# Induced attention with a max-out layer: the softmax over tokens moved ahead, its maxima sent through DRAM, its sums kept running

## The chip, the core and the metric

The kernel runs on one core of a Trainium2 chip. That core has five engines with a queue of their own each: TensorE (PE in the profile; its weight loads are listed apart as PEld), VectorE (DVE), ScalarE (ACT), GpSimd (POOL) and SyncE (SP). SP issues every DMA of this kernel, strictly in the order of its queue. All numbers are device microseconds (us) of one execution; less is better.

## The reference

`x` holds 4 batches of 12544 tokens with 128 channels, `inducing` 32 vectors of 128 channels. Cut to what is computed:

```
scale = 1 / sqrt(128)
# phase 1, one batch: 32 induced rows look at all 12544 tokens
s = scale * (inducing @ x.T);  a = softmax(s, over the tokens);  h = a @ x        # h: 32 x 128
# phase 2, every token looks at the 32 rows
s = scale * (x @ h.T);         p = softmax(s, over the 32 rows); y = p @ h
# max-out layer
z = max(y @ w1, y @ w2, y @ w3)                                                   # 768 wide
out = z @ w_out
```

All of it is float32.

## The kernel before

**Tiles.** A batch is 98 tiles of 128 tokens: one short group (group 0) of 2 tiles and six full groups (1 to 6) of 16. The four partition quarters of 32 hold four tiles side by side, so a group's 32 x tokens scores fill one PSUM bank of 128 x 512.

**Phase 1 of a group** (`attend_...`, lines 256 to 334): scores of the induced rows into `bank_a[1]` (L263, four products that sit in four column quarters of TensorE); the negated maximum of each partition on VectorE (L273); the four quarters' maxima are brought together by ScalarE (a 128x4 column, L280) and a small TensorE product with `sel` (L287), and VectorE takes the least (L291); then exp with its sum (L297, ScalarE), a 32x32 transpose (L311, VectorE), sixteen small products with the token tiles `xg` (L321) and a copy to `hg` (L334, ScalarE). Each group has a maximum of its own. After the seventh group the groups are rescaled and joined: L402 to L412, the product of the sums (L439), one product for each group (L423), the quotient (L443 to L449), and then U, which is the state times the weight differences `wcat` (L490, two banks, two column halves). U is split into a high and a low part and put into rows by four DMAs (L510); it is `us` below.

**Phase 2 of a group** (`scores_products`, `scores_steps`): scores (L525) into `bank_a[0]`, and ten steps on VectorE and ScalarE to the probabilities `ph` and `pl`, which DMAs (L591) put into `pT`, four for each chunk of 512 tokens.

**The main loop** goes over 600 slots: 4 batches x 25 chunks (a short one of 256 tokens, then 24 of 512) x 6 blocks of the 768 wide layer. A slot has two products for the layer (L606 into `pu`, L612 into `pv`), a relu on ScalarE (L621), a maximum on VectorE (L639), a rounded copy `hi` on ScalarE (L628), the rest `lo` on GpSimd or, in a few slots, on VectorE (L636, L642), and six slots later three products with `w_out` (L662 to L664). The first slot of a chunk has one more (L661), the last is followed by a copy and a DMA out (L669, L670).

**What sets the order.** All engines are ordered by hand. `at(s, f, ...)` puts a call into `plan[s]`, and `main` runs slot by slot: `advance()` (layer products), the `pT` loads, the copy out, the plan of the slot, then `stage2`. So work that is planned between two slots stands in each engine's queue exactly there. A window is 24 slots, the four chunks of a full group; window g of batch b starts at slot `150 b + 6 + 24 (g - 1)`. In the main loop of batch b the plan interleaves phase 2 of the next group and phase 1 of batch b + 1: at slots 2 and 15 of a window TensorE gets a burst of the products for both (the functions `burst` and `softmax1` set the steps, `LATE` shifts some of them by 12 slots). In windows 1 and 4 two groups of phase 1 are started, in windows 2, 3 and 5 one; in window 5 the groups are joined, and window 6 has the first phase 2 scores of the next batch. Phase 1 of batch 0 runs ahead of the loop, with its own order (`phase1_first`).

Tokens come as `xg` (L91) and, for batches 1 to 3, also as channels `xT` (L102); the short group's are `xgs` and `xTs`. They are tiles from rotating pools.

## Time and profile before

| what | value |
|---|---|
| median of 3 runs | 843.29 us (843.27 to 844.43) |
| profiled execution: span from the first to the last instruction | 841.7 us |
| what lies around the span, against the median run | 1.6 us |
| TensorE busy in the span | 817.0 us (97%) |
| ScalarE, GpSimd, VectorE busy | 741.3, 635.4, 630.7 us |
| before the first slot of the main loop | 56.5 us |
| mean granted TensorE clock | 0.995 |

The page gives no time of the profiled execution other than its span; the runs' median is 1.6 us longer. How to read it: busy shares are means over stages, and matmuls are pipelined, so that a busy TensorE says little by itself. The chain of waits follows the work that ended last back to its start; where it runs through TensorE without a break, each piece of it is time that TensorE was given for one instruction before the next could start.

### The profile page before, as it was taken

To read this page: it belongs to the slowest core of one execution; us is meant where nothing else is said; L and a number is where in the kernel's file an instruction comes from. 1 tells how busy PE (TensorE), PEld (TensorE's weight loads), DVE (VectorE), ACT (ScalarE), POOL (GpSimd) and SP (SyncE) were. 2 spreads that over 40 slices of the span, in tenths; PEclk is the share of its full clock that TensorE was granted. 3 is DMA by queue.
4 is the path that set the end of the run, shared out by engine and by line. 5 is a ranking of instruction groups with operands and counts; after the bars stand their busy time and mean duration, and the time that the engine had idled before them with its cause. 6 is when DMAs were issued, how large, how long until landed. Compare 5 with 4: busy or idle time off the path is not lost.

```text
span 841.7 us, 14677 instructions
## 1 busy us (share of the span) xinstructions
PE 817.0 (97%) x4608; PEld 635.9 (76%) x4608; DVE 630.7 (75%) x1076; ACT 741.3 (88%) x1547; POOL 635.4 (75%) x512
## 2 busy tenths in 40 slices
PE   6879999999999999999999999999999999999998
PEld 4647778777787777777777777877768878778786
DVE  5868778777686777777787778777868778777864
ACT  5759889898798998988799889889879999999996
POOL 0039778778597787877778878878759888888887
PEclk9989999999999999999999999999999999999999
DMA  9734624433425345244332462432222222222221
GB/s 348 267 96 155 219 76 157 169 116 103 146 66 175 126 157 173 70 164 158 114 92 76 162 216 70 163 122 58 64 77 81 79 75 69 64 70 76 72 79 51
DMA packets 42717, 102.50 MB, mean 122 GB/s; under 512 B 8976, under 2 KB 11152, under 8 KB 37392
## 3 DMA queue, kind: packets, MB, share of 16 engines
q1 hardware_dynamic: 42640, 101.57, 37.3%
q8 instruction: 37, 0.61, 0.3%
q14 instruction: 40, 0.33, 0.1%
HBM read 48.12 MB, written 25.69 MB: 88 GB/s over the span
## 4 chain that ended last, share of the span: by engine, by line
PE 92%; DMA 3%; DVE 2%; ACT 1%; issue 1%; SPq 0%; ACTq 0%; DVEq 0%
PE acc L662 17%; PE acc L663 16%; PE acc L664 16%; PE pu L606 16%; PE pv L612 16%; PE acc L661 3%; PE aux L525 3%; PE acc L321 2%; DMA xg<-in_x_dram 2%; PE aux L263 2%; DMA xTs<-in_xt_dram 1%; PE aux L490 1%; PE aux L423 1%; ACT ru L621 0%; PE acc L287 0%
## 5 line engine op out<-in xcount | busy, mean ns | idle before, releaser
L636 POOL TENSOR_TENSOR lo<-h,hi 128x512 fp32r<-128x512 f32 (+1 forms) x498 | 629.5, 1296 | 153.6 <-ACT hi L628 100.5
L639 DVE TENSOR_TENSOR h<-pv,ru 128x512 f32<-128x512 f32 (+1 forms) x600 | 404.5, 675 | 188.0 <-PE pv L612 122.6
L621 ACT ACTIVATE ru<-pu 128x512 f32<-128x512 f32 (+1 forms) x600 | 375.8, 626 | 73.8 <-PE pu L606 70.7
L628 ACT CAST hi<-h 128x512 fp32r<-128x512 f32 (+1 forms) x600 | 386.9, 645 | 0.3 <-DVE h L639 0.3
L662 PE MATMUL acc<-hi,wo_hi 128*128 128x512 f32 (+1 forms) x600 | 238.4, 397 | 0.0
L606 PE MATMUL pu<-pT,us 128*128 128x512 f32 (+1 forms) x600 | 232.7, 388 | 3.4 <-ACT hi L628 1.2
L612 PE MATMUL pv<-pT,us 128*128 128x512 f32 (+1 forms) x600 | 233.4, 389 | 0.0
L663 PE MATMUL acc<-hi,wo_lo 128*128 128x512 f32 (+1 forms) x600 | 232.0, 387 | 0.0
L664 PE MATMUL acc<-lo,wo_hi 128*128 128x512 f32 (+1 forms) x600 | 231.8, 386 | 0.0
L662 PEld LDWEIGHTS acc<-hi,wo_hi 128*128 128x128 f32 x600 | 113.2, 189 | 43.0 <-issue 22.0
L606 PEld LDWEIGHTS pu<-pT,us 128*128 128x128 f32 x600 | 113.2, 189 | 26.9 <-POOL us L479 2.0
L612 PEld LDWEIGHTS pv<-pT,us 128*128 128x128 f32 x600 | 113.4, 189 | 23.8 <-DVE h L639 1.3
L664 PEld LDWEIGHTS acc<-lo,wo_hi 128*128 128x128 f32 x600 | 113.0, 188 | 23.0
L663 PEld LDWEIGHTS acc<-hi,wo_lo 128*128 128x128 f32 x600 | 113.3, 189 | 20.6
L642 DVE TENSOR_TENSOR lo<-h,hi 128x512 fp32r<-128x512 f32 x102 | 72.4, 710 | 0.8 <-ACT hi L628 0.8
L669 ACT COPY o<-acc 128x512 f32<-128x512 f32 (+1 forms) x100 | 61.6, 616 | 3.1 <-PE acc L664 3.1
L661 PE MATMUL acc<-pT,us 128*128 128x512 f32 (+1 forms) x100 | 38.7, 387 | 0.0
L321 PEld LDWEIGHTS acc<-xg,aT 128*32 128x32 f32 x768 | 20.5, 110 | 13.9 <-ACT ru L621 5.7
L219 POOL TENSOR_TENSOR wo_lo<-wf,wo_hi 128x768 fp32r<-128x768 f32 x1 | 1.8, 1809 | 37.5 <-ACT wo_hi L218 37.5
L263 PE MATMUL aux<-xT,iT 128*32 128x512 f32 x192 | 25.9, 596 | 1.6 <-ACT xT L255 1.6
L321 PE MATMUL acc<-xg,aT 128*32 128x128 f32 x768 | 25.8, 274 | 1.5 <-DVE aT L311 1.1
L525 PE MATMUL aux<-xT,hT 128*32 128x512 f32 x192 | 25.6, 604 | 0.0
(101 smaller groups left out, 438.6 us busy)
## 6 DMA issues: line engine op xcount, KB each, us to landing
out_dram<-o SPq DMA_DIRECT2D x96, 256.0 KB, 2.0
xg<-in_x_dram SPq DMA_DIRECT2D x23, 1024.0 KB, 7.3
xT<-in_xt_dram SPq DMA_DIRECT2D x18, 1024.0 KB, 5.3
pT<-ph SPq DMA_DIRECT2D x192, 64.0 KB, 2.0
pT<-pl SPq DMA_DIRECT2D x192, 64.0 KB, 2.0
raw<-in_w_dram SPq DMA_DIRECT2D x3, 768.0 KB, 12.0
us<-uh SPq DMA_DIRECT2D x6, 208.0 KB, 3.1
us<-ul SPq DMA_DIRECT2D x6, 208.0 KB, 3.7
```

The costliest lines, as they stand in the source:

```text
L321: nc.tensor.matmul(out=hps[q * M : (q + 1) * M, :C], lhsT=aT[:, t * M : (t + 1) * M], rhs=xg[:, t, :], start=(t < NQ), stop=(t + NQ >= nt),)
L606: nc.tensor.matmul(out=pu[:, :w], lhsT=state[c.b]["us"][:, 2 * j * P : (2 * j + 1) * P], rhs=c.pT[:, :w], start=True, stop=True)
L612: nc.tensor.matmul(out=pv[:, : d.w], lhsT=state[d.b]["us"][:, (2 * j + 1) * P : (2 * j + 2) * P], rhs=d.pT[:, : d.w], start=True, stop=True,)
L621: nc.scalar.activation(out=ru[:, :w], in_=pu[:, :w], func=AF.Relu)
L628: nc.scalar.copy(out=hi[:, : c.w], in_=h[:, : c.w])
L636: nc.gpsimd.tensor_sub(**args)
L639: nc.vector.tensor_max(out=h[:, : d.w], in0=pv[:, : d.w], in1=relus.pop(s)[:, : d.w])
L642: nc.vector.tensor_sub(**low)
L661: nc.tensor.matmul(out=c.acc[:, :w], lhsT=us[:, 2 * DF :], rhs=c.pT[:, :w], start=True, stop=False)
L662: nc.tensor.matmul(out=c.acc[:, :w], lhsT=wo_hi[:, j, :], rhs=c.hh[j][:, :w], start=False, stop=False)
L663: nc.tensor.matmul(out=c.acc[:, :w], lhsT=wo_lo[:, j, :], rhs=c.hh[j][:, :w], start=False, stop=False)
L664: nc.tensor.matmul(out=c.acc[:, :w], lhsT=wo_hi[:, j, :], rhs=c.hl[j][:, :w], start=False, stop=(j == NJ - 1))
```

## The change

- **Phase 1 is one loop of turns.** A turn is a group; the short group and group 1 are one turn (`turns`), so there are six turns for each batch. For batch 1 they start in windows 0, 0, 1, 1, 2 and 3 of batch 0 (`FIRST`, counted from 0). For batches 2 and 3 they start one in each window, beginning in the last window but one of the batch two ahead. The products of the states and U of a batch come in the last window but one ahead of it.
- **Maxima.** VectorE negates the scores into SBUF and takes their least in one instruction (L381). The 128 values of four bytes go to a DRAM tile by one DMA (L400) and are fetched from there by another (L407), so that every partition gets four; VectorE takes the least of them and of the least so far (L413). The ScalarE column and the TensorE product with `sel` are gone for batches 1 to 3.
- **Running sums.** A turn's sums are added to `hs` and `ls` on VectorE after a rescaling by `fac` (L425 on ScalarE, L458 to L470). At the end two small products remain (L477, L478).
- **U in one bank.** Four products in four column quarters, 416 wide (L635), then one copy and one subtraction, and sixteen DMAs of 32 rows in place of four of 64 (L656). The short group's scores share that bank (L673).
- **Tiles.** `xT` and `xg` are fixed tiles with free lists, eight and five of them; the constants, `wcat` and the short group's channels are places in one tile, `shelf`. For batches 2 and 3 the `xT` loads are planned 11 slots ahead of their products; token loads go out at slot 17 of the window ahead of the sums.

```diff
-    LATE = 12
+    turns = [(0, 1)] if groups[0]["nt"] < GT else [(0,), (1,)]
+    turns += [(gi,) for gi in range(2, NG)]
...
+    short_t = [place(groups[0]["nt"] * P) for i in range(2)]
+    iT = place(M)
...
+    def turn_products(b, k):
+        for gi in turns[k]:
+            w = groups[gi]["nt"] * M
+            bank = bank_a[1] if groups[gi]["nt"] == GT else spare[0][:, C : C + w]
...
+    def turn_max(b, k):
...
+            nc.vector.tensor_scalar(
+                out=a[:, at : at + w],
+                in0=bank,
+                scalar1=-1.0,
+                scalar2=None,
+                op0=ALU.mult,
+                op1=ALU.min,
+                accum_out=mq[:, i : i + 1],
+            )
...
+    def turn_send(b, k):
+        far = st[("mq", k)] = dp.tile([P], F32, name="far", tag="far"), st.pop(("mq", k))
+        nc.sync.dma_start(out=far[0].rearrange("(m q) -> q m", q=NQ), in_=far[1])
+    def turn_fetch(b, k):
+        far = st.pop(("mq", k))[0]
+        every = far.rearrange("(m q) -> m q", q=NQ).unsqueeze(0).to_broadcast([NQ, M, NQ])
+        nc.sync.dma_start(out=st["mm"][:, k, :NQ], in_=every)
+    def turn_least(b, k):
+        nc.vector.tensor_reduce(out=st["mm"][:, k + 1, NQ:], in_=st["mm"][:, k, :known], axis=AX.X, op=ALU.min)
+    def turn_weights(b, k):
+        nc.scalar.activation(out=a, in_=a, func=AF.Exp, bias=least, scale=-1.0, accum_out=st["lst"][:, k : k + 1])
+        if k > 0:
+            nc.scalar.activation(
+                out=st["fac"][:, k : k + 1], in_=st["mm"][:, k, NQ:], func=AF.Exp, bias=least, scale=-1.0
+            )
...
+    def turn_keep(b, k):
+        if k == 0:
+            nc.vector.tensor_copy(out=st["hs"], in_=st["h"])
+            return
+        fac = st["fac"][:, k : k + 1]
+        nc.vector.scalar_tensor_tensor(
+            out=st["hs"], in0=st["hs"], scalar=fac, in1=st["h"], op0=ALU.mult, op1=ALU.add
+        )
...
+    def turn_totals(b, bank):
+        nc.tensor.matmul(out=st["lp"], lhsT=st["ls"].to_broadcast([P, P]), rhs=sel[:, :M], start=True, stop=True)
+        nc.tensor.matmul(out=st["sum"], lhsT=st["hs"], rhs=sel[:, :M], start=True, stop=True)
...
-        for k in range(2):
+        for k in range(NQ):
             nc.tensor.matmul(
-                out=bank[k * 2 * M : (k + 1) * 2 * M, :n],
-                lhsT=st["hT"][:, : 2 * M],
-                rhs=wcat[:, k * UH + half * n : k * UH + (half + 1) * n],
+                out=st["up"][k * M : (k + 1) * M, :],
+                lhsT=st["hT"][:, :M],
+                rhs=wcat[:, k * UQ : (k + 1) * UQ],
...
+    def turn(b, k, s):
+        at(s, turn_products, b, k)
+        at(s + 2, turn_max, b, k)
+        at(s + 4, turn_send, b, k)
+        at(s + 11, turn_fetch, b, k)
+        at(s + 19, turn_least, b, k)
+        at(s + 20, turn_weights, b, k)
+        at(s + 22, turn_transpose, b, k)
...
+    FIRST = ((0, 0), (0, 1), (1, 0), (1, 1), (2, 0), (3, 0))
+    BURST = (2, 15)
+    LOADT = ((0, 0, 0), (0, 0, 1), (0, 5, 2), (0, 15, 3), (1, 16, 4), (2, 15, 5))
+    LOADX = ((0, 4, 0), (0, 17, 1), (1, 4, 2), (1, 17, 3), (2, 17, 4), (3, 17, 5))
...
+            else:
+                i, part = NW * (n - 2) + NW - 2 + k, 0
+                then = (i + 1, part)
+                if k == 0:
+                    at(window(i - 1) + 7, start_batch, n)
+                at(window(i - 1) + 15, load_channels, n, k)
+                at(window(i) + 17, load_tokens, n, k)
+            at(window(then[0]) + BURST[then[1]], turn_sums, n, k)
+            at(window(then[0]) + BURST[then[1]] + 1, turn_keep, n, k)
+        s0 = window(NW * n - 2)
+        at(s0 + 6, turn_totals, n, bank_a[1])
...
+        at(s0 + 15, combine_products, n, bank_a[1])
+        at(s0 + 15, scores_products, n, 0, bank_a[1][:, UQ : UQ + 2 * M])
...
+        for r in range(NQ):
+            at(s0 + 18 + 2 * r, combine_rows, st, r)
```

How the order of the engines moves, at the places where the prediction counts. In the rows `xnn` counts equal instructions in a row, and `shelf` after the change stands for `iT`, `sel`, `wcat` and the short group's `xTs`.

**SP where a batch begins.** Before, at the start of batch 1, window 1 (SP, slots 0 to 6):

```order
L670 DMA out_dram<-o 128x512
L102 DMA xTs<-in_xt_dram 128x256
L102 DMA xT<-in_xt_dram 128x2048
L591 DMA pT<-ph 32x512
L591 DMA pT<-pl 32x512
L591 DMA pT<-ph 32x512
L591 DMA pT<-pl 32x512
L102 DMA xT<-in_xt_dram 128x2048
L670 DMA out_dram<-o 128x256
```

Now the same two loads, for batch 2, stand in the window ahead of the one that uses them (SP, slots 6 to 18 of the fourth window of batch 0; L400 is the send of the maxima, L407 their fetch, L820 the DMA out, L741 the `pT` loads):

```order
L400 DMA far<-mq 4x32x1
L741 DMA pT<-ph 32x512
L741 DMA pT<-pl 32x512
L741 DMA pT<-ph 32x512
L741 DMA pT<-pl 32x512
L820 DMA out_dram<-o 128x512
L407 DMA mm<-far 128x1x4
L106 DMA shelf<-in_xt_dram 128x256
L106 DMA xT_90<-in_xt_dram 128x2048
L741 DMA pT<-ph 32x512
L741 DMA pT<-pl 32x512
L741 DMA pT<-ph 32x512
```

The two loads have moved from the slot just ahead of their products to 11 slots ahead; a send and a fetch have been put between the DMAs of each turn.

**TensorE where the states of a batch are joined.** Before (PE, slots 15 to 17 of the fifth window of batch 0; L606 and L612 are the layer's products, L662 to L664 those with `w_out`):

```order
L321 MATMUL acc_86<-xg,aT 32x128 x16
L662 MATMUL acc_85<-hi,wo_hi 128x512
L663 MATMUL acc_85<-hi,wo_lo 128x512
L664 MATMUL acc_85<-lo,wo_hi 128x512
L606 MATMUL pu_82<-pT,us 128x512
L612 MATMUL pv_83<-pT,us 128x512
L439 MATMUL acc_86<-sel,l_2633 128x32
L662 MATMUL acc_85<-hi,wo_hi 128x512
L663 MATMUL acc_85<-hi,wo_lo 128x512
L664 MATMUL acc_85<-lo,wo_hi 128x512
L606 MATMUL pu_81<-pT,us 128x512
L612 MATMUL pv_84<-pT,us 128x512
```

Now (PE, slot 6 of the same window; L756 and L762 are the layer's products, L811 to L814 those with `us` and `w_out`):

```order
L756 MATMUL pu_81<-pT,us 128x512
L762 MATMUL pv_82<-pT,us 128x512
L477 MATMUL aux_79<-shelf,ls 128x32
L478 MATMUL aux_79<-shelf,hs 128x32
L811 MATMUL acc_85<-pT,us 128x512
```

The product of the sums stood one slot behind the last group's sums, in the bank that L334 reads; now two products stand four slots behind them, in `bank_a[1]`, and the seven products of L423 are gone.

**TensorE in a burst.** Now, slot 2 of the fifth window of batch 0 (PE; the first turn of batch 2):

```order
L673 MATMUL aux_78<-xT_91,hT 32x512 x4
L446 MATMUL acc_85<-xg_95,aT 32x128 x16
L363 MATMUL acc_85<-shelf 32x64 x4
L363 MATMUL aux_79<-xT_90,shelf 32x512 x4
L812 MATMUL acc_84<-hi,wo_hi 128x512
```

Scores of phase 2 (L673), the sums of the turn before (L446) and the next turn's scores (L363) stand in one burst, the short group's with them; before, the short group's stood in bursts of their own ahead of group 1's. Over the main loop TensorE has 26 bursts with such products now and had 32.

More of the change, by code (lines that the diff above doesn't have):

```diff
@@ L50 @@
     UW = 2 * DF + C
-    UH = UW // 2
+    UQ = UW // NQ
     groups = []
@@ L105, with place @@
     xg_next = {}
-    iT = const.tile([P, M], F32, name="iT")
+    xts_free = [const.tile([P, GT * P], F32, name=f"xT{i}", tag=f"xT{i}") for i in range(XTB)]
+    xgs_free = [const.tile([P, GT, C], F32, name=f"xg{i}", tag=f"xg{i}") for i in range(XB)]
+    w_space = xts_free.pop()
+    shelf = const.tile([P, UW + 2 * groups[0]["nt"] * P + 2 * P + 2 * M], F32, name="shelf")
+    shelf_at = [0]
+    def place(n):
+        shelf_at[0] += n
+        return shelf[:, shelf_at[0] - n : shelf_at[0]]
+    short_t = [place(groups[0]["nt"] * P) for i in range(2)]
+    iT = place(M)
     def load_raw(src):
@@ L121, in first_loads @@
                 raws.append(load_raw(srcs[what - NG]))
-    ident = const.tile([P, P], F32, name="ident")
+    ident = place(P)
     make_identity(nc, ident)
@@ L126 @@
     nc.vector.tensor_copy(out=ident_r, in_=ident)
-    sel = const.tile([P, P], F32, name="sel")
+    sel = place(P)
     nc.vector.tensor_reduce(
@@ L334, in attend_keep @@
         nc.scalar.copy(out=st["hg"][:parts, gi, :], in_=st["h"][:parts, :C])
+    def turn_products(b, k):
+        st = state[b]
+        banks = {}
+        for gi in turns[k]:
+            w = groups[gi]["nt"] * M
+            bank = bank_a[1] if groups[gi]["nt"] == GT else spare[0][:, C : C + w]
+            for q in range(NQ):
+                nc.tensor.matmul(
+                    out=bank[q * M : (q + 1) * M, :w],
+                    lhsT=iT,
+                    rhs=st["xT"][gi][:, q * w : (q + 1) * w],
+                    start=True,
+                    stop=True,
+                )
+            banks[gi] = bank[:, :w]
+        st[("s", k)] = banks
@@ new lines, in turn_max @@
+    def turn_max(b, k):
+        st = state[b]
+        a = wk.tile([P, WK], F32, name="a", tag="a")
+        mq = wk.tile([P, 2], F32, name="mq", tag="mq")
+        at = 0
+        for i, (gi, bank) in enumerate(st.pop(("s", k)).items()):
+            w = bank.shape[1]
+            nc.vector.tensor_scalar(
[7 more added lines that the diff above has]
+            )
+            at += w
+        if len(turns[k]) > 1:
+            nc.vector.tensor_tensor(out=mq[:, :1], in0=mq[:, :1], in1=mq[:, 1:], op=ALU.min)
+        st[("a", k)] = a[:, :at]
+        st[("mq", k)] = mq[:, :1]
@@ new lines, in turn_sums @@
+    def turn_sums(b, k):
+        st = state[b]
+        aT = st.pop(("aT", k))
+        rows = [st["xg"][gi][:, t, :] for gi in turns[k] for t in range(groups[gi]["nt"])]
+        for gi in turns[k]:
+            xg = st["xg"].pop(gi)
+            if groups[gi]["nt"] == GT:
+                xgs_free.append(xg)
+        st["h"] = spare[0][:, :C]
+        for t, row in enumerate(rows):
+            q = t % NQ
+            nc.tensor.matmul(
+                out=st["h"][q * M : (q + 1) * M, :],
+                lhsT=aT[:, t * M : (t + 1) * M],
+                rhs=row,
+                start=(t < NQ),
+                stop=(t + NQ >= len(rows)),
+            )
@@ L536, in scores_steps @@
         flat = sp[:, :w]
+        if nt < GT:
+            flat = wk.tile([P, w], F32, name="es", tag="es", bufs=1)
         ev = flat.rearrange("p (t m) -> p t m", m=M)
-        nc.vector.transpose(out=flat, in_=flat)
+        nc.vector.transpose(out=flat, in_=sp[:, :w])
         yield
@@ L795, in main @@
+    for n in range(1, B):
+        for k in range(NK):
+            i, part = FIRST[k] if n == 1 else (NW * (n - 2) + NW - 2 + k, 0)
+            turn(n, k, window(i) + BURST[part])
     def main():
```

227 lines of the change are left out of this document (106 added, 121 removed).

## The prediction

> **What bounds the kernel now.** I read the page's head and its chain first, then the stretches of the batches, then the chain piece by piece, then the waits.
>
> ```profile
> span 841.7 us, 14677 instructions
> PE 92%; DMA 3%; DVE 2%; ACT 1%; issue 1%; SPq 0%; ACTq 0%; DVEq 0%
> ```
>
> ```profile
> core 0: us, PE busy (x) PEld busy (x) DVE busy (x) ACT busy (x) POOL busy (x), PEclk, DMA share, GB/s
> 460.00:661.00 201.00, 198.24 (x1124) 154.25 (x1123) 151.05 (x260) 178.92 (x377) 158.71 (x127) 1.00 0.35 111
> 661.00:841.70 180.70, 177.16 (x802) 141.67 (x800) 135.19 (x214) 168.07 (x329) 149.56 (x116) 1.00 0.23 70
> ```
>
> The chain is TensorE for 92% of the span. Batch 2 takes 201.0 us, the last one 180.7: it runs the same layer but has no next batch whose phase 1 it must carry. So phase 1 of a batch costs about 20 us inside the loop, and the change lies in three such stretches. TensorE is idle for 2.8 us of the 201.0, so nearly everything must come from the length of TensorE's own queue, and little from waits.
>
> ```profile
> 206.32 0.23 PE pv L612
> 206.56 1.01 PE acc L321 x32
> 207.57 0.43 PE acc L662
> ...
> 210.07 0.41 PE acc L439 x2
> ...
> 211.69 1.51 PE aux L423 x14
> 213.20 0.28 PE acc L662
> ...
> 216.93 1.55 PE aux L490 x8
> 218.48 0.43 PE acc L662
> ```
>
> These are pieces of the chain (start, us). A layer product is worth 0.23; the first one behind a burst 0.43, so a burst pays 0.20 beyond its own pieces. (A product of float32 counts twice in `x`.)
>
> ```profile
> 122.83 1.00 PE aux L525 x8
> 123.83 0.87 PE acc L321 x32
> 124.70 0.86 PE aux L263 x8
> 125.56 0.43 PE acc L662
> ...
> 172.59 1.01 PE acc L321 x32
> 173.60 0.86 PE aux L263 x8
> ...
> 269.41 0.12 PE acc L287 x2
> 269.53 0.34 PE acc L662
> ...
> 293.49 1.08 PE acc L321 x32
> ```
>
> With the 0.20: a burst of all three costs 1.00 + 0.87 + 0.86 + 0.20 = 2.93, one of two 1.01 + 0.86 + 0.20 = 2.07. So a member that joins a burst costs 0.86, while sums alone cost 1.01 + 0.20 = 1.21: a burst as such costs about 0.34. The row at 293 is a burst whose transpose came late: 1.08 - 0.87 = 0.21 more.
>
> ```profile
> PE acc L439 <- ACT hg L334: 3.4, 3, 1.1
> PE aux L263 <- DMA xTs<-in_xt_dram: 2.9, 2, 1.5
> ```
>
> These are TensorE's two real stalls in the loop (us, times, longest): it waits for ScalarE's copy where a batch is joined, and for the short group's channels where a batch begins.
>
> **The change part by part.** All terms are for batches 1 to 3, as phase 1 of batch 0 keeps its code.
>
> *Channels loaded earlier.*
>
> ```profile
> DMA to landing us min/median/max: 2.3/2.5/2.6
> ```
>
> That is `xTs`. The load that was late stands 11 slots ahead now, some 13 us at 29.3 / 24 = 1.2 a slot (the last row of the windows below), against 2.5 us to land. The stall of 2.9 us goes.
>
> *Running sums.* The product of the sums no longer waits for L334; it reads what VectorE made three slots before. 3.4 us go. What could be late next is VectorE there; I allow up to 0.5 us twice in the range.
>
> *Maxima through DRAM.* 21 products with `sel` go, 0.12 + (0.34 - 0.23) = 0.23 each: 4.8 us. The two DMAs of a turn cost TensorE nothing as long as they are hidden; that cover is worked out under the third rival.
>
> *Joining.* The products of the groups go: 1.51 + 0.28 - 0.23 = 1.56, three times: 4.7 us. One small product comes for it. Two of the fourteen pieces of L423 would be 0.22; the piece of L439 as a whole, 0.41, bounds it from above. I take 0.22: 0.7 us back.
>
> *U in one bank.* Now 1.55 + 0.20 = 1.75. The new form is four column quarters as in L263, whose eight pieces take 0.86 at 512 wide; at 416 wide 0.70 in proportion. With 0.20 that is 0.90, so 0.85 less, 2.5 us for three; if it costs as much as at 512, 2.1. The short group's scores that now stand with it left another burst, which is no difference.
>
> *Fewer bursts.* 26 in place of 32, counted in the order: 6 x 0.34 = 2.0 us. Six bursts of the 293 kind, two in each batch, come from transposes at slot 25; all turns behind a full burst now transpose at slot 24, as in the row at 122.83: 6 x 0.21 = 1.3 us. (A second turn in a window is followed by its sums a whole window later.)
>
> *ScalarE and VectorE.* They are next in line, so their loads decide whether TensorE's shorter queue is worth its length.
>
> ```profile
> L334 ACT COPY hg<-acc 128x128 f32<-128x128 f32 x24 | 6.4, 267 | 2.0 <-PE acc L321 1.7
> L639 DVE TENSOR_TENSOR h<-pv,ru 128x256 f32<-128x256 f32 x24 | 10.1, 422 | 8.2 <-PE pv L612 5.8 <-ACT o L669 2.2
> L291 DVE TENSOR_REDUCE mneg<-acc 128x1 f32<-128x4 f32 x28 | 4.3, 153 | 1.2 <-PE acc L287 1.2
> ```
>
> ```profile
> 123.00:154.30 31.30, 31.30 (x178) 24.73 (x174) 23.87 (x40) 28.66 (x60) 25.33 (x20) 1.00 0.42 135
> 692.20:721.50 29.30, 29.30 (x136) 23.37 (x132) 23.01 (x38) 27.92 (x56) 24.49 (x19) 1.00 0.25 72
> ```
>
> For each turn ScalarE loses the copy to `hg`, 0.27, and the 128x4 column of L280; it gains one short exponential for `fac`, which I set against that column. VectorE gains the running sums: 128 columns, below the 0.42 of 256 columns and above the 0.15 of L291, so about 0.28, and a single column at 0.15, together 0.43. The negation with its minimum has the width of the old maximum, and I price it the same. In the two rows above (a window with a turn; one of the last batch, without) TensorE is busy without a gap, with ScalarE busy for 28.66 of 31.30 and for 27.92 of 29.30. With the turn's spread product gone the first becomes 31.07 long, ScalarE falls to 28.4 and VectorE rises to 24.3. ScalarE has been through a fuller window (95%) without costing TensorE anything. VectorE's 0.43 stands in slot 3, right behind the burst of 2.9 us in which it has no new products to read. I cost both at nothing; without that cover it is 0.43 for each of 18 turns, 7.7 us.
>
> **The sum.** 2.9 + 3.4 + 4.8 + 4.7 - 0.7 + 2.5 + 2.0 + 1.3 = 20.9 us. The profiled execution's span is 841.7, so 820.8 afterwards; the median of the runs is 843.3, 1.6 above that span, and with the same 1.6 the forecast is 822.4, told as **822 us**. The 56.5 us ahead of the loop keep their work and their first twelve DMAs; three token loads leave that stretch and one channel load comes, for which I allow 1 us either way. U at its dearer price and the two stalls of 0.5 add 1.4; the short group's products, no longer in bursts of their own, may save 1 us that I left out. That gives 819 to 825 for this case alone.
>
> **The rivals.**
>
> *VectorE or the transposes are late.* VectorE is in order, and slots 3 to 5 hold, beside the `h` of each slot, a transpose, two maxima over a group and now the running sums as well: that is the densest stretch of its queue. Against it: VectorE is busy for 24 of 31 us, and it has the burst to catch up. If the 0.43 shows in every turn: 822 + 7.7 = 830. Milder: the 16 bursts with scores and sums all look like the row at 293, which costs 16 x 0.21 = 3.4: 826.
>
> *The waits only move.* The constants and the short group's channels now are places in one tile. Were a load of channels to wait for the last reader of any of them, it would be issued late again and the 2.9 us stay; the three slots' distance from the running sums to the totals could be too short, and half of the 3.4 us stay: 822 + 2.9 + 1.7 = 827. Against it: the load stands early in SP's queue in the order above.
>
> *The maxima's way through DRAM stops SP: slower.* The fetch stands in SP's queue until the send has landed, and every `pT` load stands behind it.
>
> ```profile
> 301.72 0.34 SPq L670 DMA_DIRECT2D out_dram<-o  x1
> 308.94 0.35 SPq L670 DMA_DIRECT2D out_dram<-o  x1
> ```
>
> The send is issued right behind the first of such a pair, the fetch right behind the second: 7.2 us of cover. The next four `pT` loads stand eight slots ahead of their use, 9.5 us, of which their issue and landing take some 5.5, so about 4 us more are free. From a landing of 11 us on, each us costs a us in each of 18 turns, and the gain is gone at 11 + 20.9 / 18 = 12.2 us. At 12.3 us it would be 822 + 23 = 845, at 14 us 876. What speaks against it are the nearest rows (KB each, median us to landing):
>
> ```profile
> out_dram<-o SPq DMA_DIRECT2D x96, 256.0 KB, 2.0
> xg<-in_x_dram SPq DMA_DIRECT2D x23, 1024.0 KB, 7.3
> ```
>
> A write to DRAM of 256 KB lands in 2.0 us, a load of a megabyte in 7.3. No row has pieces of four bytes. I bound the send by 2.0 alone and 2.0 + 7.3 = 9.3 behind such a load, and take the low end, since no load stands shortly ahead of it in batches 2 and 3. Both ends are under 11. The Trainium skill speaks for this rival: its page "DMA: Bandwidth & Descriptors", section "Specifications", says that below 512 B the DMA engines read, modify and write, and its section "Latency and other measured facts" gives DRAM accesses 0.2 us on average and 2 us at high load. With 128 pieces on 16 engines, eight in a row each, that makes an estimate, from that page, of 2 to 16 us. No run here shows it.
>
> **How the numbers follow.** The forecast has 0.74, the late VectorE or transposes 0.12, waits that only move 0.06; all three are faster. The stopped SP has 0.05, and 0.03 are for something that gives the whole gain back without more. A difference below 0.2%, 1.7 us, can't be told from no change here. So faster 0.92, same 0.03, slower 0.05. The range runs from 817 (the lower end of the forecast, with 2 us for prices that I set too high) to 830 (VectorE late in every turn).
>
> **What would show it.** In the chain of the changed kernel the pieces at a full burst stay at 1.00, 0.87, 0.86 and 0.43; U has eight pieces of about 0.7 us; no DMA and no ScalarE row ends a wait of TensorE in the loop. Batches 0, 1 and 2 now carry eight, six and four turns: batch 1 takes about 201 - 7 = 194 us, batch 0 two turns of 0.86 + 0.87 more, batch 2 as much less, and batch 3 stays near 180.7. The send's landing stands in the DMA list: under 7 us it is hidden. A new wait of TensorE for VectorE at the totals or behind slot 3, or of SP at the fetch, would make me wrong, and so would a lower granted clock.

## The result and the profile after

The changed kernel takes 871.7 us (median of 862.3, 871.5, 871.8 and 872.9), the kernel before 843.8 in the same comparison: a ratio of 1.030 (95% interval 1.025 to 1.035). It is slower by 28 us where 822 had been forecast. The profiled execution has a span of 870.0 us. Two executions further down, one of the kernel before (1169.9 us, with a mean granted clock of 0.654) and one of the flat send (853.0 us, 0.986), lie far above the others of their kernel, and the ratios leave them out.

The head of the page of the changed kernel, and its chain by engine:

```profile
span 870.0 us, 14626 instructions
PE 61%; DMA 20%; ACT 10%; DVE 5%; SPq 2%; issue 2%; POOL 0%; DVEq 0%; ACTq 0%; POOLq 0%
```

Before, TensorE held 92% of the chain and DMA 3%. Now a fifth of it is DMA. The waits of TensorE, ScalarE and SP's queue in the changed kernel (us, times, longest), those that were not there before:

```profile
PE pu L756 <- DMA pT<-pl: 17.5, 11, 2.4
PE pu L756 <- ACT ru L771: 11.3, 6, 3.0
ACT o L819 <- DMA out_dram<-o: 18.1, 13, 3.3
ACT ph L718 <- DMA pT<-ph: 5.0, 6, 2.8
SPq L407 <- DMA far<-mq: 19.2, 15, 3.6
SPq L741 <- DMA xT<-in_xt_dram: 16.1, 9, 2.2
```

TensorE's first layer product (L756) waits for the probabilities in `pT`, and for ScalarE; ScalarE waits at the copy out (L819) for an earlier output DMA and at `ph` (L718) for an earlier `pT` load. SP stands at the fetch for the send, 19.2 us in 15 of 18 turns. The last row is a second kind of wait, at `pT` loads, which don't use what `xT` brings. Every DMA raises one of eight semaphores, strictly in turn (in this trace each of 617 issues has the semaphore of the one eight issues ahead), and it is issued only when the DMA that had the semaphore last has landed. So at most eight DMAs are under way, and SP stops at the eighth issue behind a late one. Counted in the trace, these stops take 31.4 us in the loop, 23 times; in the kernel before there are none.

Pieces of the chain of the changed kernel around two stalls of TensorE (start, us, what), then SP's queue ahead of the second stall.

```profile
304.89 6.84 DMA pT<-pl
...
311.86 0.47 PE pu L756
...
327.92 6.64 DMA pT<-ph
...
339.03 6.52 DMA pT<-pl
...
345.68 0.47 PE pu L756
```

```profile
325.60 0.34 SPq L820 DMA_DIRECT2D out_dram<-o  x1
326.04 0.59 SPq L400 DMA_DIRECT2D far<-mq  x1
326.72 0.52 SPq L741 DMA_DIRECT2D pT<-ph  x1
327.29 0.58 SPq L741 DMA_DIRECT2D pT<-pl  x1
...
334.07 0.58 SPq L407 DMA_DIRECT2D mm<-far  x1
334.70 0.47 SPq L106 DMA_DIRECT2D xT<-in_xt_dram  x1
336.08 2.27 SPq L741 DMA_DIRECT2D pT<-pl  x1
```

A `pT` load takes 6.5 to 6.8 us in the chain, 2.0 at the median before. The one of 327.92 is issued behind the send of 326.04, the one of 339.03 behind the fetch of 334.07 and a load of channels of 1024 KB. The trace also has the times at which each DMA raised its semaphore. A DMA that is spread over all sixteen DMA engines raises it sixteen times. For the send of 326.04 and its neighbours (us from the span's start; the trace lacks some increments of the `pT` loads):

```
issued 325.60 out_dram<-o   16 increments, 327.45 to 327.61
issued 326.04 far<-mq       327.03, then 332.68  333.11  333.96  334.01
issued 326.72 pT<-ph        12 increments, 328.52 to 328.65, the others from 332.85 on
issued 327.29 pT<-pl        12 increments, 329.13 to 329.26, the others from 333.03 on
```

The send's one early and four late increments show that it runs on four engines; it needs 8.0 us there. Of each `pT` load behind it twelve parts are in after 1.9 us, as always, and the four parts on those engines only when the send is through. Behind the fetch and the load of channels no part of the `pT` load of 335.35 is in before 340.63. The load of channels, issued at 334.70, lands at 344.14, 9.4 us later (5.3 at the median before); a `pT` load that needs its semaphore goes out at 344.16.

TensorE's time in the loop, in four stretches from the first layer product of a batch to that of the next. Before:

```profile
50.20:251.20 201.00, 197.31 (x1102) 152.82 (x1103) 152.05 (x264) 178.65 (x378) 156.90 (x126) 0.98 0.42 136
251.20:452.40 201.20, 198.55 (x1124) 154.53 (x1124) 151.12 (x261) 179.11 (x379) 158.94 (x128) 1.00 0.41 132
452.40:653.70 201.30, 198.54 (x1124) 154.51 (x1123) 151.04 (x261) 179.10 (x379) 158.96 (x128) 1.00 0.35 111
653.70:841.70 188.00, 184.46 (x839) 147.87 (x838) 139.78 (x223) 174.35 (x346) 156.54 (x123) 1.00 0.24 70
```

After:

```profile
54.90:268.90 214.00, 200.90 (x1136) 151.46 (x1137) 157.60 (x287) 179.93 (x366) 156.81 (x124) 0.98 0.46 141
268.90:485.90 217.00, 200.49 (x1098) 154.31 (x1097) 154.75 (x273) 179.83 (x366) 157.63 (x128) 0.98 0.42 126
485.90:682.00 196.10, 191.32 (x1039) 149.47 (x1038) 153.24 (x262) 177.28 (x363) 157.41 (x127) 1.00 0.36 108
682.00:870.00 188.00, 184.43 (x839) 147.72 (x837) 139.80 (x223) 174.14 (x345) 156.46 (x123) 1.00 0.23 70
```

The stretch without turns (the last) is unchanged at 188.0. With eight turns, six and four, the others took 13.0 and 15.8 us more and 5.2 less. TensorE is idle for 13.1 us of the first and 16.5 of the second (3.7 and 2.7 before). Part of its longer busy time is its clock: behind five idle stretches of 2.2 to 3.0 us in the loop the granted clock is at half for 3.4 us each, as in this row; behind others, of 1.4 to 2.4 us, it is not (PEclk is the third number from the right).

```profile
276.40:279.80 3.40, 3.40 (x11) 2.83 (x10) 1.00 (x3) 1.93 (x6) 2.30 (x4) 0.51 0.47 127
```

### The profile page after: what moved, and what is told of

It is laid out like the page before. It is cut to its first block, busy times and chain, and to the rows that moved or that the text cites. A ratio compares the mean times of both kernels' runs of the same rounds, so it can differ in the third digit from the quotient of the medians.

```text
span 870.0 us, 14626 instructions
## 1 busy us (share of the span) xinstructions
PE 819.8 (94%) x4530; PEld 631.8 (73%) x4530; DVE 642.9 (74%) x1112; ACT 741.5 (85%) x1508; POOL 632.3 (73%) x509
## 4 chain that ended last, share of the span: by engine, by line
PE 61%; DMA 20%; ACT 10%; DVE 5%; SPq 2%; issue 2%; POOL 0%; DVEq 0%; ACTq 0%; POOLq 0%
PE pu L756 11%; PE acc L812 11%; PE pv L762 10%; PE acc L813 10%; PE acc L814 10%; DMA pT<-pl 8%; DMA pT<-ph 6%; DMA out_dram<-o 4%; ACT ru L771 4%; ACT hi L778 3%; PE aux L673 3%; DMA xg<-in_x_dram 2%; SPq L741 2%; PE acc L446 2%; PE acc L811 2%; PE aux L363 2%
## 5 line engine op out<-in xcount | busy, mean ns | idle before, releaser
L771 ACT ACTIVATE ru<-pu 128x512 f32<-128x512 f32 (+1 forms) x600 | 369.9, 616 | 63.7 <-PE pu L756 60.1
L778 ACT CAST hi<-h 128x512 fp32r<-128x512 f32 (+1 forms) x600 | 380.6, 634 | 6.9 <-DVE h L789 6.4
L756 PE MATMUL pu<-pT,us 128*128 128x512 f32 (+1 forms) x600 | 236.0, 394 | 32.2 <-DMA pT<-pl 17.5
L762 PE MATMUL pv<-pT,us 128*128 128x512 f32 (+1 forms) x600 | 234.8, 391 | 1.9 <-DVE h L789 1.9
L814 PE MATMUL acc<-lo,wo_hi 128*128 128x512 f32 (+1 forms) x600 | 232.8, 388 | 0.0
L756 PEld LDWEIGHTS pu<-pT,us 128*128 128x128 f32 x600 | 113.9, 190 | 63.9 <-ACT ru L771 15.2
L812 PEld LDWEIGHTS acc<-hi,wo_hi 128*128 128x128 f32 x600 | 114.0, 190 | 43.4 <-issue 20.9
L762 PEld LDWEIGHTS pv<-pT,us 128*128 128x128 f32 x600 | 114.2, 190 | 27.6 <-DVE h L789 6.2
L814 PEld LDWEIGHTS acc<-lo,wo_hi 128*128 128x128 f32 x600 | 113.8, 190 | 23.5
L819 ACT COPY o<-acc 128x512 f32<-128x512 f32 (+1 forms) x100 | 60.2, 602 | 21.2 <-DMA out_dram<-o 18.1
L811 PE MATMUL acc<-pT,us 128*128 128x512 f32 (+1 forms) x100 | 39.4, 394 | 0.0
L234 POOL TENSOR_TENSOR wo_lo<-xT,wo_hi 128x768 fp32r<-128x768 f32 x1 | 1.8, 1808 | 37.7 <-ACT wo_hi L233 37.7
L673 PE MATMUL aux<-xT,hT 128*32 128x512 f32 x192 | 26.4, 623 | 0.0
L721 DVE TENSOR_TENSOR pl<-aux,ph 128x512 fp32r<-128x512 f32 x24 | 16.5, 688 | 9.9 <-ACT ph L718 9.6
L446 PEld LDWEIGHTS acc<-xg,aT 128*32 128x32 f32 x576 | 16.6, 110 | 8.8 <-issue 4.8
L718 ACT CAST ph<-aux 128x512 fp32r<-128x512 f32 x24 | 14.9, 621 | 9.3 <-DMA pT<-ph 5.0
```

What stands on the lines that cost most here:

```text
L756: nc.tensor.matmul(out=pu[:, :w], lhsT=state[c.b]["us"][:, 2 * j * P : (2 * j + 1) * P], rhs=c.pT[:, :w], start=True, stop=True)
L762: nc.tensor.matmul(out=pv[:, : d.w], lhsT=state[d.b]["us"][:, (2 * j + 1) * P : (2 * j + 2) * P], rhs=d.pT[:, : d.w], start=True, stop=True,)
L771: nc.scalar.activation(out=ru[:, :w], in_=pu[:, :w], func=AF.Relu)
L778: nc.scalar.copy(out=hi[:, : c.w], in_=h[:, : c.w])
L811: nc.tensor.matmul(out=c.acc[:, :w], lhsT=us[:, 2 * DF :], rhs=c.pT[:, :w], start=True, stop=False)
L812: nc.tensor.matmul(out=c.acc[:, :w], lhsT=wo_hi[:, j, :], rhs=c.hh[j][:, :w], start=False, stop=False)
```

## The experiments

All times are device us beside the kernel before on the same chip (845.3 beside no_exchange, fetch_only, send_only and split, which have one run each; medians of 843.1 to 843.7 beside the others). "Landing" is the last of a transfer's increments after its issue, the median over the loop; the column of `pT<-ph` gives the landing that one load in ten exceeds; for a transfer in four DMAs the landing is that of one of them. "Start" is the first layer product in the profiled execution and "loop" the time from there to its end. The start ranges from 50.2 to 57.8 us with no order in it, though the work ahead of it has neither send nor fetch of a turn; so what lies in the loop is compared by the loop, of one profiled execution each. Other runs of the same kernel can differ: the changed kernel took 862.3 to 872.9 us, both_nodep 856.8 and 867.7. The experiments in the order of the text:

```
kernel          send  fetch  pT<-ph  start    loop     us
before            -     -     3.2     50.2   791.5   843.3
no_exchange       -     -     3.9     50.4   773.8   826.0
fetch_only        -    2.6    4.9     56.4   772.2   830.3
send_only        8.1    -     7.4     54.8   790.6   847.2
both_nodep       8.2   4.2    7.9     57.8   808.1   862.3
after            8.2   6.9    8.3     54.9   815.1   871.7
fetch_late       8.1   5.5    7.2     53.5   799.9   853.3
split            3.8   1.7    5.3     55.7   777.6   835.0
send_flat        7.6    -     7.2     50.4   784.6   837.0
send_spaced      1.8    -     3.8     53.6   772.6   828.0
send_wide        1.8    -     3.9     51.8   772.5   826.1
apart_512        2.0   2.0    4.7     51.0   773.6   826.2
apart_64         2.1   2.0    4.4     53.9   773.2   828.4
pe_spread         -     -     4.1     52.1   777.7   831.4
rows             1.5    -     3.9     51.3   782.2   834.4
before_extra     8.3   3.2    7.8     50.4   818.5   868.7
```

**Is it the exchange at all?** Send and fetch are taken out, and each quarter uses its own maximum (the exchange between the quarters is left out):

```diff
-        at(s + 4, turn_send, b, k)
-        at(s + 11, turn_fetch, b, k)
```

> The changed kernel without the send and the fetch: each quarter of the partitions uses its own maximum, so the exchange between the quarters is left out and nothing else. Theory A (the two DMAs of small pieces hold up the DMA engines, and the pT loads behind them): the loss is gone, and the sum of the prediction stands, about 822 us. Theory B (SP stands at the fetch until the send has landed, and issues the pT loads too late): about 822 as well. Theory C (the added work of ScalarE and VectorE, the sixteen row DMAs or the new order costs it): 860 or more.

826.0 us (one run), 19.3 less than before, and the chain is TensorE's again:

```profile
PE 90%; DVE 3%; ACT 2%; DMA 2%; issue 1%; POOL 0%; SPq 0%; DVEq 0%; ACTq 0%; POOLq 0%
```

So the whole loss comes from the exchange: 45.6 us, of which 815.1 - 773.8 = 41.3 lie in the loop. The rest of the change does about what was forecast: the span falls by 841.7 - 824.3 = 17.4 us.

**Which of the two transfers?** Into the kernel without an exchange, the fetch alone (from a DRAM tile that was written once; its values are not used), and the send alone (nobody waits for it):

```diff
+        at(s + 11, turn_fetch, b, k)     # fetch_only: from far0, written once
+        at(s + 4, turn_send, b, k)       # send_only
```

> As no_exchange, with the fetch of each turn put back at its place; it reads a DRAM tile that was written once at the start, so SP never waits for it, and its values are not used. Theory A: the fetch's small pieces take some 7 us on 4 of the 16 engines, the pT loads behind it come late in most turns; at least 10 us more than no_exchange. Theory B: within 2 us of no_exchange, as there is nothing to wait for.

> As no_exchange, with the send of each turn put back and nothing that waits for it. Theory A: the four pT loads right behind the send land some 6 us later than now, but have 8 slots (9.5 us); 0 to 8 us more than no_exchange, and in the semaphores 4 of 16 parts of these loads come late. Theory B: within 2 us of no_exchange.

830.3 and 847.2, one run each. The send costs far more than the 0 to 8 us that its dearer expectation allowed. The 4.3 us of the fetch are no cost in the loop: it is all in the start, as the first layer product shows, here and then in the kernel without an exchange (first and last start, us).

```profile
L753 PE MATMUL pu<-pT,us x600: 277/389/767, 56.4 to 818.5; 128*128 128x512 f32 x144, 128*128 128x256 f32 x6
```

```profile
L746 PE MATMUL pu<-pT,us x600: 274/389/767, 50.4 to 814.0; 128*128 128x512 f32 x144, 128*128 128x256 f32 x6
```

The send alone costs 790.6 - 773.8 = 16.8 us in the loop, in part by way of ScalarE, though nobody uses what is sent:

```profile
ACT ph L713 <- DMA pT<-ph: 9.0, 4, 2.7
ACT o L814 <- DMA out_dram<-o: 6.7, 3, 4.1
ACT ph L713 <- DMA out_dram<-o: 5.0, 2, 2.7
PE pu L751 <- ACT ru L766: 9.6, 5, 2.3
SPq L815 <- DMA far<-mq: 2.7, 1, 2.7
SPq L736 <- DMA far<-mq: 2.6, 1, 2.6
```

The first three are its waits of ScalarE for DMAs in the loop; the kernel without an exchange has none there. ScalarE may write `ph` or `o` again only when the DMA that reads the old contents is through, and a `pT` load has four parts behind the send. TensorE then waits for ScalarE. SP, too, waits for the send, at an output and at a `pT` load: each is the eighth issue behind it and needs its semaphore. Counted in the trace, SP stands 9.4 us in the loop at such places here, and 0.4 without an exchange.

**Is SP's wait at the fetch the rest?** One kernel has both transfers, but the fetch reads the tile that was written once, so it waits for nothing (the exchange is left out). Another is the complete kernel with the fetch four slots later:

```diff
-        at(s + 11, turn_fetch, b, k)
+        at(s + 15, turn_fetch, b, k)     # fetch_late
```

> Left out: the exchange between the quarters (each quarter uses its own maximum); the send goes out at its place and is read by nobody, the fetch at its place reads a DRAM tile that was written once before the loop, so SP never waits at the fetch, and both transfers are there. With no exchange at all the kernel took 826.0 us, with the fetch alone 830.3, with the send alone 847.2, with send and fetch as changed 871.7. Theory 'SP wait': the 24 us between the last two come from SP standing at the fetch until the send has landed; then this kernel is at 847 to 852. Theory 'engines': send and fetch fall on the same DMA engines and hold up each other and the pT pieces behind them, whether SP waits or not; then it is at 865 to 872.

> Complete computation; the changed kernel with the fetch four slots later (fifteen slots behind the products of a turn instead of eleven), so 11 slots or some 13 us lie between send and fetch where the send needs about 8 to land. Theory 'SP wait': SP no longer waits at the fetch, so the part of the loss that this wait makes goes: 847 to 852, and the profile has no wait of SP's queue at the fetch. Theory 'engines': the fetch only meets another set of transfers; 860 to 872. If VectorE now waits for the fetch at the least of the maxima, the wait shows there and the time says nothing on either.

The first took 856.8, between the two expectations, and 867.7, inside the dearer one; in the profiled one, of 867.7, the loop costs 808.1 - 773.8 = 34.3 us without SP's wait at the fetch, against 41.3. So it is not mainly that wait. SP's waits for a semaphore are still there, 22.1 us in the loop by the trace; two of their rows:

```profile
SPq L743 <- DMA xT<-in_xt_dram: 5.8, 5, 1.9
SPq L658 <- DMA xg<-in_x_dram: 4.0, 2, 2.5
```

Send alone (16.8) and fetch alone (nothing) cost twice as much together as the send does. A reading that fits, though no run isolates it, is that the fetch has its pieces on four engines too and meets a send there that isn't through: it lands in 4.2 us here and in 2.6 alone. The later fetch gave 853.3, just above 847 to 852: SP waits at it twice instead of 15 times, and 815.1 - 799.9 = 15.2 us of the loop come back, while VectorE now waits for the fetched maxima (us, times, longest):

```profile
DVE mm L413 <- DMA mm<-far: 26.3, 14, 4.3
SPq L407 <- DMA far<-mq: 5.1, 2, 2.9
```

How much of the 15.2 is SP's wait and how much the collision that the later fetch also avoids, these two don't tell. By the profiled execution of the first kernel the wait at the fetch is worth 41.3 - 34.3 = 7 us; that kernel's other run was 10.9 us shorter, so the 7 can be some 18.

**Four engines, or four bytes?** The complete kernel with both transfers cut in four by quarters, so that each has 32 rows and runs on sixteen engines; and the send alone, in the order of the partitions, as 128 rows of one value:

```diff
-        nc.sync.dma_start(out=far[0].rearrange("(m q) -> q m", q=NQ), in_=far[1])
+        for q in range(NQ):              # split
+            nc.sync.dma_start(
+                out=far[0].rearrange("(m q) -> q m", q=NQ)[q].unsqueeze(1), in_=far[1][q * M : (q + 1) * M, :]
+            )
```

```diff
-        nc.sync.dma_start(out=far.rearrange("(m q) -> q m", q=NQ), in_=state[b][("mq", k)])
+        nc.sync.dma_start(out=far.unsqueeze(1), in_=state[b][("mq", k)])      # send_flat
```

> The changed kernel with the send cut into four DMAs of 32 pieces and the fetch into four, one for each quarter, complete as to the computation. SP has 6 more issues a turn, 0.58 us each. Theory A: 32 pieces spread over all 16 engines, two on each, land in about 2.5 us and hold nothing up: 822 to 830. Theory B: the wait at the fetch is gone as well, but SP loses 3.5 us more a turn to issuing: 825 to 840. If it stays at 860 or more, it isn't the number of pieces on one engine.

> The kernel with the send alone (847.2 us; the exchange between the quarters is left out, nobody reads what is sent), with one difference: the 128 values go to DRAM in the order of the partitions, so that the transfer is 128 rows of one value and not 4 rows of 32. Same 128 pieces of four bytes, same place. Theory 'four engines': the loss comes from 32 pieces one behind the other on each of four DMA engines; laid over sixteen engines with eight each the send lands in 2 to 4 us and costs at most 4 us in all: 826 to 830. Theory 'small pieces': the number of four-byte writes sets the cost wherever they lie; 842 to 848.

835.0 (one run), and 837.0 for the flat send (836.8 and 837.0, and the 853.0 named above). The split exchange costs 3.8 us of the loop, so spreading helps; each of its four sends lands in 3.8 us, the four together in 6.2 from the first issue on. SP stands for a semaphore there too, 25.0 us in the loop, so such a wait need not cost much. But I had expected 2 to 4 us of landing for the flat send, and it was 7.6, with eight pieces on each engine instead of 32, at a price of 784.6 - 773.8 = 10.8 us. The theory that four engines are the cause of the long landing fell with that: the 128 writes take about the same time on four engines and on sixteen, which fits writes that wait for each other somewhere behind the engines. Four engines still cost the loop more, 16.8 against 10.8. Why four sends of 32 rows cost less than one of 128 stays open.

**Where the bytes go.** The flat send with its values 512 bytes apart in DRAM, and with pieces of 512 bytes side by side (rows of a constant tile, read by nobody):

```diff
-        far = dp.tile([P], F32, name="far", tag="far")
-        nc.sync.dma_start(out=far.unsqueeze(1), in_=state[b][("mq", k)])
+        far = dp.tile([P, P], F32, name="far", tag="far")
+        nc.sync.dma_start(out=far[:, :1], in_=state[b][("mq", k)])            # send_spaced
+        nc.sync.dma_start(out=far, in_=ident)                                 # send_wide
```

> The kernel with the send alone in the order of the partitions (837.0 us; the exchange between the quarters is left out), with one difference: the 128 values are written 512 bytes apart in DRAM instead of side by side. In the flat send the last of the sixteen engines reported 7.6 us after the issue (median), with eight pieces each, about as late as the 8.1 us of four engines with 32 each. Theory 'same place': the writes wait for each other because they fall on the same few lines of DRAM; spaced out they land in 2 to 4 us and the kernel takes 826 to 830. Theory 'four bytes': a write of four bytes is slow by itself, wherever it goes; the landing stays at 6 to 9 us and the kernel at 834 to 840.

> As the flat send alone (837.0 us; the exchange between the quarters is left out), but each of the 128 pieces is 512 bytes, side by side (the rows of a constant 128x128 tile; nobody reads them). Theory 'four bytes': the size of the piece is what is slow, so 64 KB in 128 pieces land like a DMA of the output, in about 2 us, and the kernel takes 826 to 829. Theory 'pieces': the number of pieces written sets the cost; the landing is 6 us or more and the kernel at 835 or above.

Both land in 1.8 us, and the kernels take 828.0 (ratio 0.981, 0.977 to 0.984) and 826.1 (0.979, 0.975 to 0.982). A write of four bytes isn't slow by itself, and 128 of them aren't too many: what is slow here is 128 small writes side by side. 7.6 us over 128 are 0.06 us each, as if they were made one after the other. (The Trainium skill, in "DMA: Bandwidth & Descriptors", section "Specifications", says that pieces under 512 B are read, modified and written. Size alone would have kept the spaced send slow, and it didn't.)

**The same in the complete kernel.** The changed kernel, with only the layout of the DRAM tile changed: the four values of a row stay together, the rows stand 512 bytes apart (or 64, with a tile of 32 x 16):

```diff
-        far = st[("mq", k)] = dp.tile([P], F32, name="far", tag="far"), st.pop(("mq", k))
-        nc.sync.dma_start(out=far[0].rearrange("(m q) -> q m", q=NQ), in_=far[1])
+        far = st[("mq", k)] = dp.tile([M, P], F32, name="far", tag="far"), st.pop(("mq", k))
+        nc.sync.dma_start(out=far[0][:, :NQ].rearrange("m q -> q m"), in_=far[1])
...
-        every = far.rearrange("(m q) -> m q", q=NQ).unsqueeze(0).to_broadcast([NQ, M, NQ])
+        every = far[:, :NQ].unsqueeze(0).to_broadcast([NQ, M, NQ])
```

> Complete computation; the changed kernel with one difference: in the DRAM tile the 16 bytes of the four quarters stand 512 bytes apart for each of the 32 rows, instead of side by side; the same four by 32 pieces of four bytes, the same fetch, the same slots. Theory 'same place': of the changed kernel's loss of 45.6 us against no exchange (826.0) nearly all comes from writes of four bytes that fall side by side; what is left are the four writes that share a row's 16 bytes and SP's issues: 826 to 833, faster than before. Theory 'four engines and a waiting fetch': 32 pieces on each of four engines and a fetch behind them go on holding up pT: 845 or more.

> As the one before, with the rows 64 bytes apart instead of 512 (2 KB in all). Theory 'same place' says nothing on how far apart is enough: if 64 bytes are, 826 to 833 as at 512; if writes within 512 bytes still wait for each other, between that and the changed kernel's 871.7, near 845.

826.2 us (ratio 0.980, 0.977 to 0.982) and 828.4 (0.982, 0.979 to 0.986). The first, whose profile follows, has the same DMAs, the same four engines, the same 32 pieces of four bytes on each, the same slots. The send lands in 2.0 us instead of 8.2, and SP's waits for a semaphore fall from 31.4 us in the loop to 1.4. Its chain, its stretches and their sum:

```profile
PE 90%; DVE 5%; ACT 2%; issue 1%; DMA 1%; POOL 0%; SPq 0%; DVEq 0%; ACTq 0%; POOLq 0%
```

```profile
51.00:251.30 200.30, 197.05 (x1136) 150.59 (x1137) 158.50 (x287) 179.27 (x367) 157.50 (x125) 0.98 0.48 153
251.30:445.70 194.40, 193.44 (x1098) 151.50 (x1097) 155.90 (x273) 177.42 (x365) 157.55 (x127) 1.00 0.43 137
445.70:636.60 190.90, 190.19 (x1039) 149.88 (x1038) 153.24 (x262) 176.53 (x363) 157.59 (x127) 1.00 0.36 111
636.60:824.50 187.90, 184.37 (x839) 147.75 (x837) 139.70 (x223) 174.15 (x345) 156.31 (x123) 1.00 0.23 70
sum 773.50, PE 765.05 PEld 599.73 DVE 607.34 ACT 707.37 POOL 628.96; mean PE 191.26 PEld 149.93 DVE 151.83 ACT 176.84 POOL 157.24
```

```profile
sum 815.10, PE 777.14 PEld 602.97 DVE 605.39 ACT 711.18 POOL 628.31; mean PE 194.29 PEld 150.74 DVE 151.35 ACT 177.80 POOL 157.08
```

The last row is the sum of the changed kernel's four stretches, quoted above. So the 870.0 - 824.6 = 45.4 us between the two are 29.5 of idle TensorE in the loop (38.0 against 8.5), 12.1 of longer busy time, to which the half clock belongs, and 3.9 ahead of the loop.

**Other ways for the maxima.** The ScalarE column and TensorE product of the kernel before, with all else of the change kept (the product stands at slot 18 of the turn, and VectorE takes the least in two instructions from the second turn on):

```diff
-        nc.sync.dma_start(out=far[0].rearrange("(m q) -> q m", q=NQ), in_=far[1])
+        md = wk.tile([P, NQ], F32, name="md", tag="md")
+        nc.scalar.mul(out=md, in_=quad, mul=far[1])
...
+        nc.tensor.matmul(out=spare[0][:, :NQ], lhsT=sel, rhs=st.pop(("mq", k)), start=True, stop=True)
```

> Complete computation; everything of the change is kept but the way through DRAM: the maxima of the quarters are brought together as before, by a ScalarE column and a TensorE product with sel. Theory: the whole loss comes from the two transfers, so this is the kernel without an exchange (826.0 us) plus 18 products of 0.23 us, 4.1 us: 828 to 831, faster than before by 1.5 to 2%. The prediction's ledger gives 822.4 + 4.1 = 826.5. The rival that the longer prefetch, the running sums or U in one bank cost something too gives more than 835.

831.4 (ratio 0.986, 0.982 to 0.990), just above the upper end of 828 to 831; the loop costs 3.9 us more than without an exchange, where 4.1 were expected. And rows of 128 bytes, transposed by VectorE, moved from SBUF to SBUF and transposed back (VectorE takes the least at slot 13 instead of 19):

```diff
+        nc.vector.transpose(out=mrow[0], in_=mcol)
...
+        part = mrow[0].rearrange("(q m) c -> q m c", m=M)[:, 0, :]
+        for q in range(NQ):
+            nc.sync.dma_start(out=mrow[1][q * M : q * M + NQ, :], in_=part)
...
+        nc.vector.transpose(out=mcol, in_=mrow[1])
```

> Complete computation, the changed kernel with another way for the maxima: VectorE transposes the column of 128 values to four rows of 32, four DMAs with four pieces of 128 bytes each bring the four rows to every quarter from SBUF to SBUF, VectorE transposes back and takes the least. No TensorE product, no DRAM, no piece of four bytes; four more issues on SP and three more small instructions on VectorE for each turn. Theory 'four bytes': sixteen larger pieces land in about 2 us and hold nothing up, so this is the kernel without an exchange, 826 us, plus what VectorE's small instructions cost if not hidden (at most 18 x 0.4 = 7 us): 826 to 833. Theory 'any transfer in SP's queue at this place costs': 840 or more, with late pT loads as in the changed kernel.

834.4 (0.988, 0.985 to 0.991), above the 826 to 833 that were expected. The transfers land in 1.5 us, and no DMA ends a wait of TensorE or ScalarE in the loop. Of the 782.2 - 773.8 = 8.4 us of the loop 3.1 are idle TensorE, which waits at ten places for VectorE's `h` instead of three (1.9 us without an exchange). The other 5.2 are longer busy time of TensorE, and no run shows why. Its waits for `h`:

```profile
PE pv L762 <- DVE h L789: 5.0, 10, 0.7
```

**The exchange put into the kernel before**, unused, for its 21 groups:

```diff
+        at(s + 4, extra_send, b)
+        at(s + 11, extra_fetch, b)
```

> The kernel before, unchanged in its computation, with a send and a fetch in the changed kernel's form added to each of the 21 groups of its phase 1 in the loop, at the same distances (4 and 11 slots behind the products); nobody uses what is fetched, the fetch waits for its send. If the two transfers are the whole loss, whatever the kernel around them: 843.5 + 18 to 21 x 2.5 (45.6 us over 18 turns, the changed kernel against the one with no exchange) = 885 to 896. If it needs the tighter schedule of the changed kernel, in which TensorE leaves less room: under 865.

868.7 (ratio 1.029, 1.024 to 1.033): 27.0 us in the loop, 1.3 for each group where the changed kernel pays 41.3 / 18 = 2.3 for each turn. It lies between the two expectations. The loss doesn't need the changed kernel, and it is higher there.

## Why the prediction was wrong

**The step that failed** is in the part on the maxima through DRAM: "The two DMAs of a turn cost TensorE nothing as long as they are hidden". The landing itself was inside the bounds, 8.2 us between 2.0 and 9.3, though I took the low end, 2.0; by the third rival's working nothing is lost below 11. But that working counts one thing only, when SP comes past the fetch. What stands behind the *send* was not counted: four `pT` loads and the next output go out right behind it, to the same sixteen engines. Of the loads the parts on the send's four engines are late, and SP stops at the eighth issue behind a late DMA. The send alone cost 16.8 us in the loop, where the prediction had nothing, and 34.3 together with a fetch that waits for nothing. How much of this is late data, late release of `ph` and `o`, and SP's stops, no run separates; that the 128 writes side by side are at the root is shown, since moving them 64 or 512 bytes apart takes the loss away.

The third rival had the right place and sign. Its mechanism, SP standing at the fetch, is there (19.2 us), but it is the smaller part, some 7 us of 41.3, at most some 18, by the kernel whose fetch waits for nothing, and the loss came at a landing of 8.2 us, not from 12.2 on. It had nothing of SP's stops for a semaphore. Nor were "128 pieces on 16 engines, eight in a row" right: the trace shows four engines.

Two rules of the page "DMA: Bandwidth & Descriptors" of the Trainium skill speak of this, and the prediction didn't weigh them. "Why a DMA increments its semaphore by 16 and not by 1" says that the slowest dimension sets how many engines a DMA uses, here 4; the send's first increment and its four late ones agree. "Queues, rings and completion order" says that an engine's increment lands only after every earlier write of that engine; the twelve `pT` parts in time and the four late ones agree.

**The ledger of TensorE held for the most part**, as the complete kernel with the rows 512 bytes apart shows. The forecast saved 20.9 us on the span; it saves 841.7 - 824.6 = 17.1.

- The load of channels: the wait of 2.9 us for `xTs` is gone. The product of the sums: the 3.4 us for ScalarE are gone; the two new products wait twice for VectorE, 0.5 in all.
- Added up over the loop, the time that TensorE's bursts and small products add to its layer products (from the end of the product ahead of each to the end of the one behind it, less the 0.227 us of a plain one) is 89.7 us before and 68.4 now: 21.3 saved, against 20.9. A full burst costs 2.93, as forecast; U with the short group's scores 1.15, where 0.90 was forecast for U alone.
- The stretches: batch 1 takes 194.4 (forecast about 194), batch 2 190.9 (about 190.5), the last 187.9, and 188.0 before. The prediction's 180.7 for the last batch was cut at 661.0, but that batch's first layer product stands at 653.7; so a batch with a next one to carry takes 201.3 - 188.0 = 13.3 us more, not about 20 (no term of the sum uses this). In the same way its 56.5 us ahead of the loop are 50.2 to the first layer product. Batch 0 was to take 197.5 and takes 200.3. That is 2.8 of the missing 3.8 us, and why is not shown; the loop begins 0.8 later.
- VectorE's running sums were mis-sized. 128 columns take 0.31 us (0.28 forecast), but the single column 0.70, not 0.15:

```profile
L464 DVE SCALAR_TENSOR_TENSOR ls<-ls,fac,lst 128x1 f32<-128x1 f32 x12 | 8.4, 702 | 0.0
L461 DVE SCALAR_TENSOR_TENSOR hs<-hs,fac,acc 128x128 f32<-128x128 f32 x15 | 4.6, 309 | 0.0
```

```profile
PE pv L762 <- DVE h L789: 1.9, 3, 0.7
PE aux L477 <- DVE a L381: 0.5, 2, 0.3
```

  These are groups of instructions (count | busy us, mean ns) and waits of TensorE in the kernel with the rows 512 bytes apart. So a turn costs VectorE 1.0 us there instead of 0.43, and the cover still held in most turns: TensorE waits for VectorE for 2.4 us in the loop, where the first rival had 7.7.

What the prediction named as the signs of its own failure did show: a landing of the send above 7 us, DMA and ScalarE rows that end a wait of TensorE in the loop, a wait of SP at the fetch, a lower granted clock (0.982 against 0.995).

## What to carry to other kernels

A DMA that nobody waits for still has a price: count what is issued behind it, on the engines that it occupies, until it has landed, and count how many DMAs the program lets its queue have under way (eight here). Small values that go to DRAM are better not packed side by side: here, with the rows of the tile 64 or 512 bytes apart the same 128 writes landed in 2 us instead of 8. Where a wide price hides under "it is covered", ask for every queue that the work shares, not only for the one that waits in the program.

## What was not expected of the hardware

- 128 writes of four bytes into 512 neighbouring bytes of DRAM took 7.6 us on sixteen engines and 8.1 on four; 512 bytes apart, 1.8 us. That they are made one after the other at that place is a reading that fits these times; which part of the chip does it, no run shows.
- A DMA issued while four engines are behind can be late on all sixteen: the output of 332.82 raised its semaphore from 336.88 to 337.50, the one of 325.60 within 2.0 us. Why all of them, stays open.
- The start of the loop, after nearly the same work, ranged from 50.2 to 57.8 us over the profiled executions. In the changed kernel's trace TensorE's clock was at half from 40.9 to 51.2 us. What causes it is open; up to 7.6 us between single times above can be this.
